# A pair's two heads in 64-row tiles of the array: scores and transposes of an attention and token-mixer kernel

## Chip, cores, metric

One Trainium2 chip, one core. The metric is the device time of one execution in microseconds (us), the median of several runs. TensorE is called PE in the profile (its weight loads PEld), VectorE DVE, ScalarE ACT, GpSimd POOL, SyncE SP.

## What is computed

q, k and v have shape (4, 8, 576, 64): four batches of eight heads, 576 positions, head size 64, fp32. The reference rotates q and k by position, takes softmax attention per head, lays the heads side by side to x of shape (4, 576, 512) and runs a token mixer and a channel mixer over it:

```python
scores = scale * np.matmul(q_rot, k_rot.transpose(0, 1, 3, 2))
scores = scores - np.max(scores, axis=-1, keepdims=True)
attn = np.exp(scores)
attn = attn / (np.sum(attn, axis=-1, keepdims=True) + 1e-09)
out = np.matmul(attn, v)
...
h = np.maximum(xt @ w_tok1, 0.0) @ w_tok2
u = x + h.transpose(0, 2, 1)
out = u + np.maximum(u @ w_ch1, 0.0) @ w_ch2
```

The mixer weights arrive as 64-bit floats and are split on the chip into rounded part and rest.

## The kernel before

The work on attention goes in 16 pairs of heads (n = 0 to 15); a pair's two heads fill the 128 partitions with 2 x 64 head columns. 576 = 512 + 64: each head has four blocks of 128 queries and a tail of 64.

`prep(n)` (from line 248) loads k, q and v of a pair (lines 258 to 265), rotates k and q (line 273; on POOL, for the first pair on DVE) and transposes them on PE: five 128x128 transposes each, lines 314 and 316. ACT writes the rounded part in fp32r from PSUM (kh, qh, line 319), DVE the rest (kl, ql, line 322). Both heads lie on top of each other then, head 0 in partitions 0 to 63, head 1 in 64 to 127. The score product wants the contraction of one head on all 128 rows: eight transfers of a pair on SP's queue (line 352) stack copies, khd = [kh; kh], kld = [kl; kl] and qs = [qh; ql] for each head. The first pair writes head 0's copies directly (lines 332 and 335).

`pair(n)` (line 385) walks nine tiles in the order of line 381: eight (head, query block) tiles and one tile (None) that holds both heads' 64 tail queries. Per tile:

- scores (line 423): four matmuls of 288 columns, (qh + ql) against kh and kl, into a score buffer of two PSUM banks; the None tile (line 414) does six against a block-diagonal bd that POOL fills (line 375);
- maximum on DVE (line 428), exponential with its sum on ACT (line 435), to p of 576 columns;
- four 128x128 transposes of p (line 445) into one PSUM bank, copied to pt by ACT or DVE (lines 453 and 455); the 64 tail columns of several tiles are transposed together later (line 465) and copied (line 485).

There are two score buffers of two banks each and four single banks for everything else, which makes up PSUM's eight banks. Twice in a pair, P times V (line 498) follows: ten fp32 products, each of which shows as two matmuls, the two heads in the lower and the upper 64 output columns of the array. The result oT is copied out (line 502), transposed back (lines 528 and 531), copied to X by ACT (line 537) and multiplied by the reciprocal sums on POOL (line 547); its 64-row tail goes through DVE (line 540).

The order of the work on each engine is fixed ahead by `Plan.run` (line 89): a list scheduler with planned durations, lags between engines and a rank from the table AT (line 144); of the tasks that can start within SLACK of the earliest one, the lowest rank goes first. A task takes its buffers when it is placed; score buffers are taken in program order. Engines then run their queues strictly in that order. The splitting of the token weights (lines 567 to 603) is spread over the first pairs on DVE, ACT and POOL. After attention come the token mixer (lines 700 and 722) and the channel mixer (lines 761, 783 and 806), which the change does not touch.

## Time and profile before

| | |
|---|---|
| median of 3 runs | 694.57 us (692.72 to 695.56) |
| the profiled execution | 693.52 us, of which the span from first to last instruction is 691.7 us |
| mean granted TensorE clock | 0.994 |
| busy share of the span | PE 95%, PEld 81%, DVE 62%, ACT 47%, POOL 42% |
| first and last P times V of attention | start at 31.6 us and 314.8 us |
| first matmul of the channel mixer's line 783 | 381.7 us |

Busy shares are unions of instruction times. Matmuls are pipelined: one that is listed with 0.3 us may be followed 0.13 us later by the next, so its cost is read from the distance of starts or from the chain of waits. The chain of waits follows the work that ended last back from the end; "issue" in it is time in which nothing recorded held the engine.

### The profile page before, as it was taken

What the parts mean: (1) busy time and instruction counts of PE and PEld (TensorE: products, weight loads), DVE (VectorE), ACT (ScalarE), POOL (GpSimd) and SP (SyncE); (2) the same over time, 40 slices, a digit from 0 to 9 for tenths busy, and PEclk for the clock granted to TensorE, in tenths of its full rate; (3) what the DMA queues carried; (4) which work ended last, traced back from release to release, by engine and by line L of the source; (5) the groups of instructions that cost most, each with busy time, mean ns of one, the idle gap of its engine ahead of it and who ended that gap; (6) DMA issues with size and microseconds to landing.
All of it is one profiled execution on the core that took longest, in us unless ns stands there. A gap on an engine that the chain in (4) does not pass through costs nothing.

```text
span 691.7 us, 11124 instructions
## 1 busy us (share of the span) xinstructions
PE 660.6 (95%) x4024; PEld 557.4 (81%) x4024; DVE 429.1 (62%) x739; ACT 324.9 (47%) x755; POOL 292.7 (42%) x314
## 2 busy tenths in 40 slices
PE   2898999999999999997999999999999999999997
PEld 1766778877777777775887989989989899899895
DVE  5789976666666666656884888727842673322322
ACT  3776777767667777764551535313411321011010
POOL 4887976666666665102832545503600340000000
PEclk9999999999999999998999999999999999999999
DMA  7665555555556654420300223202200100001212
GB/s 221 157 177 148 137 145 137 139 149 151 151 151 151 151 149 119 112 74 1 98 17 1 69 85 84 69 0 85 69 30 1 62 0 1 1 0 47 77 61 92
DMA packets 43127, 61.75 MB, mean 89 GB/s; under 512 B 11584, under 2 KB 24640, under 8 KB 43072
## 3 DMA queue, kind: packets, MB, share of 16 engines
q1 hardware_dynamic: 42528, 60.38, 32.1%
q8 instruction: 32, 0.52, 0.3%
q10 hardware_dynamic: 544, 0.66, 0.3%
q14 instruction: 23, 0.19, 0.1%
HBM read 29.88 MB, written 4.72 MB: 50 GB/s over the span
## 4 chain that ended last, share of the span: by engine, by line
PE 81%; ACT 6%; DVE 5%; issue 4%; DMA 2%; SPq 0%; POOL 0%; ACTq 0%; DVEq 0%; POOLq 0%
PE m L783 22%; PE m L806 22%; PE t L498 10%; PE s L423 7%; PE t L445 6%; PE m L700 4%; PE m L722 4%; ACT p L435 3%; DVE nm L428 2%; ACT pt L455 2%; PE s L414 2%; PE t L465 2%; PE m L761 1%; PE t L528 1%; PE t L314 1%
## 5 line engine op out<-in xcount | busy, mean ns | idle before, releaser
L428 DVE TENSOR_REDUCE nm<-s 128x1 f32<-128x576 f32 x144 | 106.6, 749 | 45.0 <-PE s L423 36.7
L785 ACT ACTIVATE gh<-m 128x384 fp32r<-128x384 f32 x72 | 35.4, 492 | 190.9 <-PE m L783 174.7
L435 ACT ACTIVATE p<-s,nm 128x576 f32<-128x576 f32 x144 | 106.9, 744 | 30.0 <-DVE nm L428 27.5
L783 PE MATMUL m<-uh,c1h 128*128 128x384 f32 x288 | 97.1, 337 | 0.0
L783 PE MATMUL m<-uh,c1l 128*128 128x384 f32 x288 | 96.7, 336 | 0.0
L783 PE MATMUL m<-ul,c1h 128*128 128x384 f32 x288 | 96.7, 336 | 0.0
L423 PE MATMUL s<-khd,qs 128*128 128x288 f32 x256 | 83.2, 341 | 5.1 <-ACT p L435 4.2
L498 PE MATMUL t<-pt,vraw 128*64 128x256 f32 (+1 forms) x640 | 85.6, 411 | 0.2 <-ACT pt L455 0.2
L806 PE MATMUL m<-c2h,gl 128*128 128x512 f32 x216 | 85.2, 394 | 0.0
L806 PE MATMUL m<-c2l,gh 128*128 128x512 f32 x216 | 85.0, 394 | 0.0
L806 PE MATMUL m<-c2h,gh 128*128 128x512 f32 x216 | 84.9, 393 | 0.0
L787 DVE SCALAR_TENSOR_TENSOR gl<-m,gh 128x384 fp32r<-128x384 f32 x72 | 39.6, 555 | 70.4 <-ACT gh L785 70.3
L808 DVE TENSOR_TENSOR X<-m,X 128x512 f32<-128x512 f32 x64 | 44.1, 690 | 58.6 <-PE m L806 58.6
L445 PE MATMUL t<-ident,p 128*128 128x128 f32 x576 | 77.5, 275 | 0.7 <-DVE XT L540 0.4
L423 PE MATMUL s<-kld,qs 128*128 128x288 f32 x256 | 72.7, 300 | 0.0
L498 PEld LDWEIGHTS t<-pt,vraw 128*64 128x64 f32 x640 | 44.0, 137 | 31.3 <-issue 5.1
L445 PEld LDWEIGHTS t<-ident,p 128*128 128x128 f32 x576 | 66.7, 141 | 2.1 <-DVE XT L540 0.9
L423 PEld LDWEIGHTS s<-khd,qs 128*128 128x128 f32 x256 | 49.3, 192 | 20.6 <-ACT p L435 12.8
L783 PEld LDWEIGHTS m<-uh,c1h 128*128 128x128 f32 x288 | 54.2, 188 | 0.9
L783 PEld LDWEIGHTS m<-ul,c1h 128*128 128x128 f32 x288 | 54.2, 188 | 0.9
L783 PEld LDWEIGHTS m<-uh,c1l 128*128 128x128 f32 x288 | 54.2, 188 | 0.0
L592 POOL TENSOR_TENSOR fa<-fc,fa 128x384 f32<-128x384 f32 (+1 forms) x23 | 27.7, 1207 | 57.7 <-DVE fa L590 57.7
(128 smaller groups left out, 1234.7 us busy)
## 6 DMA issues: line engine op xcount, KB each, us to landing
khd<-kh SPq DMA_DIRECT2D x62, 144.0 KB, 2.6
kld<-kl SPq DMA_DIRECT2D x62, 144.0 KB, 2.7
stg<-in_moe_w_ch_dram SPq DMA_DIRECT2D x16, 384.0 KB, 3.2
stg<-in_moe_w_ch_dram SPq DMA_DIRECT2D x12, 512.0 KB, 3.6
kraw<-in_k_dram SPq DMA_DIRECT2D x16, 256.0 KB, 2.9
qraw<-in_q_dram SPq DMA_DIRECT2D x16, 256.0 KB, 3.1
vraw<-in_v_dram SPq DMA_DIRECT2D x16, 256.0 KB, 3.0
out_dram<-X SPq DMA_DIRECT2D x16, 256.0 KB, 2.3
```

Source lines behind the costliest of these rows:

```text
L423: nc.tensor.matmul(sb.t[:, c, 0:W2], a, m.t[:, h, c * W2:(c + 1) * W2], start=(x == 0), stop=(x == 1))
L428: nc.vector.tensor_reduce(out=nm.t, in_=sb.t[:, :, 0:W2], axis=AX.XY, op=ALU.max, negate=True)
L435: nc.scalar.activation(out=p.t.rearrange("p (a b) -> p a b", a=2), in_=sb.t[:, :, 0:W2], func=ACTF.Exp, bias=nm.t, accum_out=l)
L445: nc.tensor.transpose(tb.t[:, j * P:(j + 1) * P], p.t[:, j * P:(j + 1) * P], ident)
L498: nc.tensor.matmul(ab.t[h * D:(h + 1) * D, 0:w], vb.t[:, h, r, :], pt[c].t[:, r, h, 0:w], start=(r == 0), stop=(r == R))
L592: mul_ = lambda e: lambda: e.tensor_tensor(out=A(), in0=C(), in1=A(), op=ALU.mult)
L700: nc.tensor.matmul(tb.t, a, m, start=(r == 0 and i == 0), stop=(r == R and i == len(lst) - 1))
L783: nc.tensor.matmul(tb.t[:, 0:N], a, m, start=(i == 0), stop=(i == len(lst) - 1))
L785: x = add("ACT", 0.49, lambda f=f, tb=tb: nc.scalar.activation(out=gb.t[0][:, f], in_=tb.t[:, 0:N], func=ACTF.Relu), [x], [tb, gb], pr + f)
L787: y = add("DVE", 0.56, lambda f=f, tb=tb: nc.vector.scalar_tensor_tensor(out=gb.t[1][:, f], in0=tb.t[:, 0:N], scalar=0.0, in1=gb.t[0][:, f ...
L806: nc.tensor.matmul(tb.t, a, m, start=(i == 0), stop=(i == len(lst) - 1))
L808: y = add("DVE", 0.69, lambda u=u, tb=tb: nc.vector.tensor_tensor(out=u, in0=tb.t, in1=u, op=ALU.add), [z] + sums.get((ci, x), []), [tb], ...
```

## The change

Head 0 lies in the upper 64 rows and head 1 in the lower 64 rows of kh, kl, qh and ql, and the scores are now computed from there, each head in its own 64-row tile of the array, with three products (qh kh, qh kl, ql kh) in place of the stacked two matmuls. One task (0.8 us in the plan) computes the block of 128 queries for both heads: 12 matmuls of 288 columns, head 0 and head 1 alternating, into both score buffers. khd, kld, qs and their transfers are gone; kh, kl, qh and ql have two buffers each.

All transposes of attention (k and q, p, oT) are done as two half transposes, rows 0 to 63 and rows 64 to 127, each of 128 stationary columns against a 64x64 identity, into two PSUM banks; what was one bank and one copy becomes two banks and two copies of 64-column blocks. The key blocks are laid out so that head 0's tail keys and head 1's tail keys are neighbours: p of both heads is one tile of 1152 columns, and the block of both tails is transposed with head 1's. k's and q's 64 tail rows are loaded into both partition halves, v's into one half per head with zeros in the other. The final multiplication by the reciprocal sums is done by DVE out of PSUM; ACT's copy and POOL's multiplication go.

The plan gets a mode per PE task (full, row or col) and 0.15 us where the mode changes. The None tile's scores stay in full mode.

```diff
+        want = {}
...
-                if not sl.free or (sl.fifo and b.order != sl.taken):
+                k = want[sl] = want.get(sl, -1) + 1
+                if len(sl.free) <= k or (sl.fifo and b.order != sl.taken + k):
                     return None
-                s = max(s, min(sl.free)[0])
+                s = max(s, sorted(sl.free)[k][0])
+        if eng == "PE" and t.mode != self.mode:
+            s = max(s, self.clock["PE"] + SWITCH)
         return s
...
+            if eng == "PE":
+                self.mode = t.mode
...
+SWITCH = 0.15
...
-        hls = {x: slots(x, 1, [P, S], F32R) for x in ("kh", "kl", "qh", "ql")}
-        khds = slots("khd", 2, [P, 2, S], F32R)
-        klds = slots("kld", 2, [P, 2, S], F32R)
-        qss = slots("qs", 2, [P, 2, M], F32R)
+        hls = {x: slots(x, 2, [P, 2 * R + 2, TL], F32R) for x in ("kh", "kl", "qh", "ql")}
         bds = slots("bd", 2, [P, 2, P], F32R)
-        ps = slots("p", 4, [P, S])
-        pts = slots("pt", 3, [P, R + 1, 2, 2 * P + TL])
-        oTs = slots("oT", 2, [P, S])
+        ps = slots("p", 3, [P, 2 * S])
+        pqs = slots("pq", 1, [P, S + TL])
+        pts = slots("pt", 3, [P, 2 * R + 1, 2 * P + TL])
+        oTs = slots("oT", 2, [P, M + P])
...
+        for j in range(4):
+            nc.scalar.dma_start(out=tabs[TL:P, j, R], in_=tab[j, 0:TL, R])
...
-                def dup(dst, o, h, src, w):
-                    def go():
-                        nc.sync.dma_start(out=dst.t[o * D:(o + 1) * D, h, 0:w].bitcast(F32),
-                                          in_=src.t[h * D:(h + 1) * D, 0:w].bitcast(F32))
...
+                    xy = [Buf(t_ps), Buf(t_ps)]
+
+                    split = r0 > 0
+                    first = int(n > 0)
+
+                    def tr(r0=r0, r1=r1, xy=xy, ub=ub, first=first):
+                        for i in range(r1 - r0):
+                            for z in range(2):
+                                r = (i - 1) % (R + 1) if z and first else r0 + i
+                                nc.tensor.transpose(xy[z].t[:, i * TL:(i + 1) * TL],
+                                                    ub.t[halves[z], r].rearrange("p h d -> p (h d)"), ident[halves[z], halves[z]])
+
+                    pp = pos + AT["pt"] + pr if n else FIRST + r0
+                    t = add("PE", 0.11 * (r1 - r0), tr, x, [*xy, ub, hi, lo], pp, mode="row")
+                    for z in range(2):
+                        m = r1 - r0 - (z and split)
+                        i0 = 0 if z and first else 2 * r0 + z + 1
+                        parts = [(0, m, i0)] + ([(m, 1, 0)] if z and split else [])
+                        for o, m, i0 in parts:
+                            src = lambda z=z, xy=xy, m=m, o=o: xy[z].t[:, o * TL:(o + m) * TL].rearrange("p (r s) -> p r s", s=TL)
+                            at = lambda d, i0=i0, m=m: d.t[:, i0:i0 + 2 * m - 1:2]
+
+                            def fh(hi=hi, src=src, at=at):
+                                nc.scalar.copy(out=at(hi), in_=src())
+
+                            def fl(hi=hi, lo=lo, src=src, at=at):
+                                nc.vector.tensor_tensor(out=at(lo), in0=src(), in1=at(hi), op=ALU.subtract)
+
+                            y = add("ACT", act(m * TL), fh, [t], [xy[z], hi], pp)
+                            eh.append(y)
+                            el.append(add("DVE", dve(m * TL), fl, [y], [xy[z], hi, lo], pp))
+                ready[n, nm] = (eh + el, hi, lo)
...
+                                nc.gpsimd.tensor_copy(out=bb.t[halves[h], o, halves[h]], in_=src.t[halves[h], 2 * R + 1])
+                            bdone.append(add("POOL", 0.3, cp, eh + el, [bb, src], pp))
...
-        ORDER = [(0, 0), (1, 0), (0, 1), (1, 1), None, (0, 2), (1, 2), (0, 3), (1, 3)]
-        ORDER0 = [(0, 0), (0, 1), (0, 2), (0, 3), (1, 0), (1, 1), None, (1, 2), (1, 3)]
+        ORDER = [0, 1, None, 2, 3]
...
+            for i, j in enumerate(ORDER):
+                g = 9 * n + 2 * i
+                c = 0 if j in (0, 1) else 1
+                if j is None:
...
+                                nc.tensor.matmul(sb.t[:, c, 0:W2], a, flat(m.t)[:, TL + c * W2:TL + (c + 1) * W2], start=(x == 0), stop=(x == 2))
+                    x = add("PE", 0.81, qk, bdone + kd, [sb, bb, kh, kl], g + AT["qkt"])
...
+                    def tr(pb=pb, xy=xy):
+                        for r in range(R + 1):
+                            for z in range(2):
+                                c0 = r * P - (TL if z and r == R else 0)
+                                nc.tensor.transpose(xy[z].t[:, r * TL:(r + 1) * TL], pb.t[halves[z], c0:c0 + P], ident[halves[z], halves[z]])
+
+                    x = order_tr[0] = add("PE", 0.55, tr, [*x, order_tr[0]], [*xy, pb, pt[c]], g + AT["tr"], mode="row")
+                    y = None
+                    for z in range(2):
+                        def cp(e, z=z, xy=xy, c=c, m=R + 1 - z):
+                            return lambda: e(out=pt[c].t[:, (R + 1) * z:(R + 1) * z + m, 2 * P:2 * P + TL],
+                                             in_=xy[z].t[:, 0:m * TL].rearrange("p (r s) -> p r s", r=m))
+
+                        y0, y = y, both(cp, (R + 1 - z) * TL, [x], [xy[z], pt[c]], g + AT["cp"])
+                        ev[c].append(y)
+
+                    def cpt(e, xy=xy, c=c):
+                        return lambda: e(out=pt[c].t[halves[1], R, 2 * P:2 * P + TL], in_=xy[1].t[halves[1], R * TL:(R + 1) * TL])
+                    ev[c].append(both(cpt, TL, [x, y0], [xy[1], pt[c]], g + AT["cp"]))
...
+                sbs, nmb, pb = [Buf(s_ps), Buf(s_ps)], [Buf(nms), Buf(nms)], Buf(ps)
+
+                def qk(sbs=sbs, j=j):
+                    for c in range(2):
+                        for x, (a, m) in enumerate(((qh, kh), (qh, kl), (ql, kh))):
+                            for h in range(2):
+                                nc.tensor.matmul(sbs[h].t[:, c, 0:W2], flat(a.t)[halves[h], TL + j * P:TL + (j + 1) * P],
+                                                 flat(m.t)[halves[h], TL * (1 - h) + c * W2:TL * (1 - h) + (c + 1) * W2], start=(x == 0), stop=(x == 2))
+                t = add("PE", 0.8, qk, qd + kd, [*sbs, qh, ql, kh, kl], g + AT["qk"], mode="row")
+                xs = []
+                for h in range(2):
+                    x = add("DVE", 0.67, mx(sbs[h], nmb[h]), [t], [sbs[h], nmb[h]], g + h + AT["mx"])
+                    x = add("ACT", 0.65, ex(sbs[h], nmb[h], lambda h=h, pb=pb: pb.t[:, h * S:(h + 1) * S], lambda h=h, j=j: lb.t[:, j, h:h + 1]), [x],
+                            [sbs[h], nmb[h], pb, lb], g + h + AT["ex"])
+                    xs.append(x)
+                exps += xs
+                o = j % 2 * P
+
+                for h in range(2):
+                    xy = [Buf(t_ps), Buf(t_ps)]
+                    m = R + h
+
+                    def tr(pb=pb, xy=xy, h=h, m=m):
+                        for i in range(m):
+                            for z in range(2):
+                                c0 = h * M + i * P
+                                nc.tensor.transpose(xy[z].t[:, i * TL:(i + 1) * TL], pb.t[halves[z], c0:c0 + P], ident[halves[z], halves[z]])
+
+                    x = order_tr[0] = add("PE", 0.11 * m, tr, [*xs[0:h + 1], order_tr[0]], [*xy, pb, pt[c]], g + h + AT["tr"], mode="row")
+                    for z in range(2):
+                        def cp(e, z=z, xy=xy, c=c, o=o, h=h, m=m):
+                            return lambda: e(out=pt[c].t[:, R * h:R * h + m, o + z * TL:o + (z + 1) * TL],
+                                             in_=xy[z].t[:, 0:m * TL].rearrange("p (r s) -> p r s", r=m))
+                        ev[c].append(both(cp, m * TL, [x], [xy[z], pt[c]], g + h + AT["cp"]))
+                if j not in (1, 3):
...
-                            nc.tensor.matmul(ab.t[h * D:(h + 1) * D, 0:w], vb.t[:, h, r, :], pt[c].t[:, r, h, 0:w],
-                                             start=(r == 0), stop=(r == R))
+                            m = pt[c].t[:, R if r == R else r + h * (R + 1), 0:w]
+                            nc.tensor.matmul(ab.t[halves[h], 0:w], vb.t[:, h, r, :], m, start=(r == 0), stop=(r == R))
...
+                x = add("PE", 10 * (w / 1200 + 0.0025), pv, ev[c] + vdone, [ab, vb, pt[c]], g + AT["pv"], mode="col")
...
+            xy = [Buf(t_ps), Buf(t_ps)]
...
-                for j in range(R):
-                    nc.tensor.transpose(tb.t[:, j * P:(j + 1) * P], oT.t[:, j * P:(j + 1) * P], ident)
...
-            def f6():
-                nc.scalar.copy(out=xm, in_=tb.t.rearrange("p (r c) -> p r c", r=R))
...
-            def f8():
-                x4 = xm.rearrange("p r (h d) -> p r h d", h=2)
-                nc.gpsimd.tensor_tensor(out=x4, in0=x4, in1=rb.t[:, 0:R, :].unsqueeze(3).to_broadcast([P, R, 2, D]), op=ALU.mult)
...
+                for j in range(R + 1):
+                    for z in range(2):
+                        nc.tensor.transpose(xy[z].t[:, j * D:(j + 1) * D], oT.t[halves[z], j * P:(j + 1) * P], ident[halves[z], halves[z]])
+
+            x = add("PE", 0.55, f4, pv_done, [*xy, oT], pp, mode="row")
+            for z in range(2):
+                def f5(z=z):
+                    nc.vector.tensor_tensor(out=X[b][:, :, cs + z * D:cs + (z + 1) * D], in0=xy[z].t[:, 0:R * D].rearrange("p (r d) -> p r d", r=R),
+                                            in1=rb.t[:, 0:R, z].unsqueeze(2).to_broadcast([P, R, D]), op=ALU.mult)
+
+                def f6(z=z):
+                    nc.vector.tensor_tensor(out=tail_of(b)[:, cs + z * D:cs + (z + 1) * D], in0=xy[z].t[0:TL, R * D:(R + 1) * D],
+                                            in1=rb.t[0:TL, R, z:z + 1].to_broadcast([TL, D]), op=ALU.mult)
+                x_done.setdefault(b, []).append(add("DVE", dve(R * D), f5, [x, inv], [xy[z], rb], pp + AT["f6"]))
+                x_done[b].append(add("DVE", dve(D), f6, [x, inv], [xy[z], rb], pp + AT["f6"] + 0.1))
```

## Rows read from the trace of the kernel before

**Rows 1.** The page: busy time of the engines over the span.

```profile
PE 660.6 (95%) x4024; PEld 557.4 (81%) x4024; DVE 429.1 (62%) x739; ACT 324.9 (47%) x755; POOL 292.7 (42%) x314
```

**Rows 2.** Windows: length, then busy us and instructions of PE, PEld, DVE, ACT, POOL.

```profile
119.05:283.17 164.12, 162.44 (x1243) 129.16 (x1242) 107.67 (x199) 117.10 (x289) 101.86 (x124) 1.00 0.55 140
35.68:82.86 47.18, 41.94 (x305) 32.47 (x304) 43.47 (x63) 35.17 (x89) 40.02 (x40) 1.00 0.59 151
```

**Rows 3.** Chain of waits over one pair: start, us, engine, tile, line, instructions.

```profile
200.86 2.31 PE t L498 x20
203.16 1.25 PE s L423 x8
...
204.53 1.31 PE t L445 x12
...
210.47 2.84 PE t L498 x20
...
214.64 0.53 PE s L423 x4
...
219.14 0.36 PE t L498
```

**Rows 4.** Timeline of PE, first 0.34 us of one P times V.

```profile
200.78 0.44 PE L498 MATMUL t<-pt,vraw 128*64 128x256 f32 x2
```

**Rows 5.** Timeline of weight loads, the first two after P times V.

```profile
203.09 0.19 PEld L423 LDWEIGHTS s<-khd,qs 128*128 128x128 f32 x1 [0.39 <-issue]
...
203.20 0.19 PEld L423 LDWEIGHTS s<-kld,qs 128*128 128x128 f32 x1
```

**Rows 6.** Timelines: the hand-offs from scores to maximum, exponential and next scores.

```profile
297.89 0.40 PE L423 MATMUL s<-khd,qs 128*128 128x288 f32 x1 [0.19 <-ACT p L435]
...
298.40 0.29 PE L423 MATMUL s<-kld,qs 128*128 128x288 f32 x1
...
298.80 0.76 DVE L428 TENSOR_REDUCE nm<-s 128x1 f32<-128x576 f32 x1 [0.23 <-ACT pt L455]
...
299.59 0.74 ACT L435 ACTIVATE p<-s,nm 128x576 f32<-128x576 f32 x1
...
215.85 1.43 DVE L428 TENSOR_REDUCE nm<-s 128x1 f32<-128x576 f32 x2
...
289.46 0.74 ACT L435 ACTIVATE p<-s,nm 128x576 f32<-128x576 f32 x1 [0.46 <-DVE nm L428]
...
290.34 0.19 PEld L423 LDWEIGHTS s<-khd,qs 128*128 128x128 f32 x1
```

**Rows 7.** Groups by form, ACT and DVE: count, busy us, mean ns, idle before.

```profile
L455 ACT COPY pt<-t 128x512 f32<-128x512 f32 x63 | 35.2, 588 | 4.0 <-PE t L445 3.0
...
L319 ACT CAST kh<-t 128x320 fp32r<-128x320 f32 x16 | 6.9, 432 | 0.3
...
L322 DVE TENSOR_TENSOR ql<-t,qh 128x320 fp32r<-128x320 f32 x16 | 7.8, 490 | 30.2 <-ACT qh L319 30.1
...
L322 DVE TENSOR_TENSOR ql<-t,qh 128x256 fp32r<-128x256 f32 x16 | 6.7, 421 | 2.5 <-ACT qh L319 2.4
...
L485 ACT COPY pt<-t 64x256 f32<-64x256 f32 x18 | 6.7, 370 | 1.0 <-PE t L465 0.2 <-DVE pt L485 0.2
```

**Rows 8.** Chain of waits in the first pairs.

```profile
31.17 0.59 SPq L352
...
33.47 2.55 DMA kld<-kl
```

**Rows 9.** Chain and timeline: second P times V of three pairs, then the last multiplication.

```profile
82.93 2.87 PE t L498 x20
...
283.24 2.84 PE t L498 x20
...
314.78 3.10 PE L498 MATMUL t<-pt,vraw 128*64 128x320 f32 x20
...
319.54 1.04 POOL L547 TENSOR_TENSOR X<-X,ri 128x512 f32<-128x512 f32 x1 [3.00 <-ACT X L537]
```

More of the change, by code (lines that the diff above doesn't have):

```diff
@@ L49 @@
 class Task:
-    __slots__ = ("alts", "deps", "bufs", "prio", "end", "eng", "waits", "heirs")
+    __slots__ = ("alts", "deps", "bufs", "prio", "end", "eng", "waits", "heirs", "mode")
 LAG = {"PE": 0.2, "ACT": 0.14, "DVE": 0.12, "POOL": 0.12, "SP": 1.8}
@@ L62, in __init__, with add @@
         self.slack = SLACK
-    def add(self, eng, dur, fn, deps=(), bufs=(), prio=0.0, alts=()):
+        self.mode = None
+    def add(self, eng, dur, fn, deps=(), bufs=(), prio=0.0, alts=(), mode="full"):
         t = Task()
+        t.mode = mode
         t.alts = [(eng, dur, fn)] + list(alts)
@@ L241, in attention, with both @@
             nc.gpsimd.memset(t[TL:P, R, 1:2], 1.0)
-        for _, _, t in pts.free:
-            nc.gpsimd.memset(t[TL:P, R], 0.0)
-        make_identity(nc, ident)
-        ready_q, ready_k, ready_v, kpair, bd_of = {}, {}, {}, {}, {}
+        for _, _, t in raw["v"].free:
+            nc.gpsimd.memset(t[TL:P, 0, R, :], 0.0)
+            nc.gpsimd.memset(t[0:TL, 1, R, :], 0.0)
+        for _, _, t in oTs.free:
+            nc.gpsimd.memset(t[:, S:M + P], 0.0)
+        for _, _, t in pqs.free:
+            nc.gpsimd.memset(t[:, S:S + TL], 0.0)
+        make_identity(nc, ident)
+        ready, ready_v, bd_of = {}, {}, {}
+        order_tr = [None]
+        halves = (slice(0, TL), slice(TL, P))
+        def both(fn, n, deps, bufs, prio):
+            return add("ACT", act(n), fn(nc.scalar.copy), deps, bufs, prio, alts=[("DVE", dve(n), fn(nc.vector.tensor_copy))])
         def prep(n):
@@ L250, in prep @@
             pos = 9 * n
-            hb = {}
-            last = []
             for nm, src, pr in (("k", k, 0.0), ("q", q, 0.5), ("v", v, 1.0)):
@@ L388, in pair @@
             pt = [Buf(pts) for _ in range(2)]
[L389 to L392 removed]
+            kd, kh, kl = ready[n, "k"]
+            qd, qh, ql = ready[n, "q"]
             bdone, bb = bd_of[n]
             vdone, vb = ready_v[n]
[L395 to L397 removed]
@@ L398, in pair @@
-            place = lambda t: (1, 2 * P) if tiles[t] is None else (tiles[t][1] // 2, tiles[t][1] % 2 * P)
-            ends = {max(t for t in range(9) if place(t)[0] == c): c for c in range(2)}
-            def both(fn, n, *args, prio):
-                return add("ACT", act(n), fn(nc.scalar.copy), *args, prio, alts=[("DVE", dve(n), fn(nc.vector.tensor_copy))])
+            flat = lambda t: t.rearrange("p r s -> p (r s)")
+            ev = {0: [], 1: []}
+            exps = []
             oT = Buf(oTs)
@@ L405, in pair, with mx, ex @@
             pv_done = []
-            for t in range(9):
-                g = 9 * n + t
-                sb = Buf(s_ps)
-                if tiles[t] is None:
+            def mx(sb, nm):
+                return lambda: nc.vector.tensor_reduce(out=nm.t, in_=sb.t[:, :, 0:W2], axis=AX.XY, op=ALU.max, negate=True)
+            def ex(sb, nm, p, l):
+                return lambda: nc.scalar.activation(out=p().rearrange("p (a b) -> p a b", a=2), in_=sb.t[:, :, 0:W2], func=ACTF.Exp,
+                                                    bias=nm.t, accum_out=l())
@@ L413, in qk @@
                             for x, (a, m) in enumerate(passes):
-                                nc.tensor.matmul(sb.t[:, c, 0:W2], a, m[:, c * W2:(c + 1) * W2], start=(x == 0), stop=(x == 2))
-                    x = add("PE", 0.81, qk, bdone + keh + kel, [sb, bb, khi, klo], g + AT["qk"])
-                else:
-                    h, j = tiles[t]
-                    def qk(sb=sb, h=h, j=j):
-                        a = qb.t[:, h, j * P:(j + 1) * P]
-                        for c in range(2):
-                            for x, m in enumerate((khd, kld)):
-                                nc.tensor.matmul(sb.t[:, c, 0:W2], a, m.t[:, h, c * W2:(c + 1) * W2], start=(x == 0), stop=(x == 1))
-                    x = add("PE", 0.55, qk, qdone[h] + kdone[h], [sb, qb, khd, kld], g + AT["qk"])
```

172 lines of the change are left out of this document (22 added, 150 removed).

## The prediction

> **What bounds the kernel now.** I read the page first: PE is busy for 95% of the span, no other engine for more than 62% [rows 1]. A busy PE is no proof of a bound, since matmuls overlap in the records, so the second view is the chain of waits over one pair in the even middle of attention [rows 3]. It goes from one P times V to the next in 219.14 - 200.86 = 18.28 us and consists almost wholly of PE's own work. The pitches in it are: 12 transposes in 1.31, so 0.109 each; 4 score matmuls in 0.53, so 0.133 each; P times V 2.31 and 2.84. These two differ by 0.53 for 10 x 64 columns, so 10 steps of 256 columns need 2.12, and entering this mode costs about 0.19. The eight score matmuls behind it take 1.25 where 8 x 0.133 = 1.06, so leaving it costs another 0.19.
>
> PE's work in a pair is then 32 score matmuls x 0.133 = 4.26, six of the None tile 0.80, 60 transposes (45 of p, 10 of k and q, 5 of oT) x 0.109 = 6.54, and P times V 2.31 + 2.84 + 2 x 0.19 = 5.53: together 17.13 of 18.28. PE binds, with 1.15 us of standing still in a pair. In the windows view DVE works 107.67 / 9 = 12.0 and ACT 117.10 / 9 = 13.0 us of nine such pairs [rows 2]: loaded, not full. Eleven steps of this pace lie between the second P times V of pair 3 at 82.93 and that of pair 14 at 283.24 [rows 9], 18.21 each. Before them, DVE is busy 43.47 of 47.18 us with the token weights beside attention [rows 2], and the pace is slower. The mixers behind attention are not changed.
>
> **The change part by part.**
>
> *Scores.* Four blocks of six steps replace 32 matmuls, a step being one matmul for each head. Whether the two heads run side by side in row tiles no row shows. The nearest row is P times V, whose two heads lie in column tiles: two matmuls start inside the first 0.34 us as one record of 0.44 [rows 4], and ten steps of two products take 2.31. The best case for a score step is 0.133, the streaming of 288 columns; the worst is 0.22, if two loads of 128 columns follow each other: behind P times V the second load starts 203.20 - 203.09 = 0.11 after the first [rows 5]. I take 0.133, by the column tiles: 24 x 0.133 = 3.19, a gain of 1.07.
>
> The full-size scores also show that a load and the matmul ahead of it overlap: 0.133 is less than a load of 0.11 plus 288 columns of streaming. The Trainium skill, TensorE: Matmul & The Clock Gate, section Part 3 (The mechanism), says that weight loads overlap running matmuls only when their row groups differ. The trace's full-array scores do not agree with it; by that rule alone a step would be a load and a stream in turn, an estimated 0.23, PE's work would come above 21 us a pair, and the change would lose.
>
> *Transposes.* 36 + 5 half pairs of p, 10 of k and q and 5 of oT make 56 steps for 60. A step streams half the columns (0.055 at best) but loads 128 stationary columns, 0.11 [rows 5]; the worst is 0.22. I take 0.109, the load's: 56 x 0.109 = 6.10, a gain of 0.44.
>
> *Modes.* The None tile's full-array scores now sit between row tiles. The row for a change of mode is P times V's entry and exit, 0.38 together; bounds 0 to 0.38; I take 0.38. P times V and the None scores stay.
>
> PE's work: 3.19 + 0.80 + 6.10 + 5.53 + 0.38 = 16.0, or 1.13 less than today.
>
> *The score buffers* are the new chain. A block now takes both buffers at once, so the next block waits for both exponentials. With the hand-offs of today [rows 6]: six steps until the last starts take 0.10 + 0.66 (the first pitch is longer), the maximum starts 298.80 - 298.40 = 0.40 behind the last start, two maxima take 1.43, the exponential follows a maximum at 0.03 and takes 0.74, and PE restarts 290.34 - 290.20 = 0.14 behind it. The first exponential ends at 2.69, the second at 3.43, the next block starts at 3.57. The None tile takes the first buffer that comes free, at 2.83, and needs 1.16 + 0.76 + 0.03 + 0.74 + 0.14 of its own and some 0.19 for the mode, so that the next block starts 5.85 behind the last one. A pair is 3 x 3.57 + 5.85 = 16.6 us at least. That is above PE's 16.0: score buffers, DVE and ACT become the bound.
>
> *Lateness.* Each of the five starts can be late when DVE or ACT is in a copy. Such copies take 0.43 to 0.49 [rows 7], on average half of one, 0.2, is left. 16.6 + 5 x 0.2 = 17.6; bounds 0 and a whole copy, 0.49.
>
> *Copies on ACT and DVE.* For p, nine of 512 columns (0.588) and tails of about 1.6 become 16 of 256 or 320 (0.37 and 0.43) and three for the None tile: 6.9 to 7.45. The rounded part and rest go to 320 columns throughout, +0.27. ACT's copy to X goes, -0.59; DVE takes two multiplications of 256 (0.42 each) and two of 64 (0.2, an estimate from these) for one of 128 (0.28), +0.96. Together +1.2 on 25.0 us of two engines; they have 35 in a pair, so it costs only through lateness.
>
> *Queues.* SP issues eight transfers less and three tail loads more per pair; the copies' landing matters once, in the first pair, where the chain stands from 31.17 to 36.02 on four issues and a landing [rows 8]. That is 4.8 us; DVE, full there, gets the work of the wait back and has 1 us more a pair. I take half, -2.5; bounds -4.8 and +3. Four small loads on ACT's queue at the start hide behind the first rotation. POOL's multiplication goes from the end of attention, 1.04 [rows 9] for 0.84 on DVE and no copy of 0.59: -0.8. POOL's bd copies now wait for all eight splits of q; ranks well ahead of the None tile cover it, and without that cover it is one 0.5 us start a pair, inside the lateness.
>
> *The end.* The last two steps take 314.78 - 283.24 = 31.5 us today, since there is no preparation left beside them [rows 9]. The score chain does not shrink with it: 17.6 + 16.6 = 34.2, +2.7.
>
> **The sum**: 11 x (17.6 - 18.21) = -6.7, -2.5, -0.8, +2.7: -7.3 us. Against the profiled execution's 693.52 (span 691.7) this gives 686.2; the median of the runs stands 1.05 higher, so 687.
>
> **The rivals.** *The buffer chain holds without lateness* (16.6): 11 x -1.6 = -17.7, -4.8, -0.8, +1.7: 673. For it: DVE and ACT have a quarter of their time free; the scheduler ranks scores and exponentials first. Against: PE's 16.0 must fit between the blocks without delaying one, and P times V is 3 us in one piece where a block leaves 2.7.
>
> *It is lost again in the buffers.* With a lateness of 0.33 per start (half a copy on DVE and a little on ACT) a pair is at 18.2 and only start and end differ: about 695.
>
> *Slower by the same chain.* One whole copy, 0.49, ahead of each start: 16.6 + 2.45 = 19.05, 11 x 0.84 = +9.2, end +6.5 - 0.8, first steps -2.5: 707. It decides from 0.33 on. For it: both engines run strictly in the planned order, the block's maxima and exponentials stand in it among some 27 other instructions of a pair, and the plan counts 0.67 and 0.65 for what takes 0.76 and 0.74. The Trainium skill, TensorEngine Tiling (Array Packing), section PSUM Bottleneck, says the same in general: tiling speeds up TensorE, not the emptying of PSUM, which may become the bottleneck.
>
> *The tiles do not run side by side.* 24 and 56 steps at 0.22: PE's work is 5.3 + 12.3 + 0.80 + 5.53 + 0.38 = 24.3 a pair: 11 x 6.1 = +67, +8 in the first three steps, +15 in the last two: about 784. Loads that wait for their own tile's stream end near there too (21 us a pair, some 740). Against both: the column tiles [rows 4] and the pitch of the full array [rows 3].
>
> **How the numbers follow.** Half a percent, 3.5 us, is about what a measurement of this kernel can tell from no change. Forecast and its near side (678 to 691) 0.36; the chain without lateness (under 678) 0.20; nothing to be seen (691 to 698) 0.18; slower by the chain 0.20; tiles one after the other 0.06. That gives faster 0.56, same 0.18, slower 0.26. The range goes from 668, five below the best case, since its hand-offs are single rows, to 708, the slower chain: some 0.15 is left out, most of it above. The likeliest cases' own range is 673 to 691.
>
> **What would show it.** Right: pairs of score matmuls of the two heads that start within 0.01 us, a step of 0.13, transposes at 0.11 per two; PE's gaps ahead of scores ended by ACT's exponential, some 3.6 to 4 us apart; a pair at 17 to 18 us; no transfers of khd, kld and qs. Wrong: a score step of 0.22 or more; a pair under 16.6, which would mean that scores started without waiting for both buffers; PE still without gaps.

## The result, and the profile after

The change makes the kernel **slower by 0.9%**: 699.51 us median (696.52 to 701.61, 13 runs) against 693.07 (691.86 to 695.56, 13 runs) of the kernel before in the same comparison, ratio 1.0086, 95% interval 1.0071 to 1.0101. The forecast was 687. The profiled execution after took 696.52 us, span 694.7, where that of before took 693.52 and 691.7: the traces differ by 3.0 of the 6.4 us.

The edit also gives the new kernel another rank table AT and other values of SLACK ("qk" goes from -1.07 to -239.14, for example), which the section on the change does not say. So the 0.9% belongs to row tiles and another order together, and only the runs below that choose the order anew on both sides take the two apart.

The page first, the line that answers to [rows 1]:

```profile
PE 630.0 (91%) x5112; PEld 529.2 (76%) x5112; DVE 432.4 (62%) x807; ACT 319.8 (46%) x808; POOL 282.1 (41%) x304
```

PE's busy time went down by 30 us and no other engine's went up by more than 3.3. The windows view over nine even pairs, and over the two steps from the second P times V of pair 1 to that of pair 3, for [rows 2]:

```profile
119.87:285.55 165.68, 145.07 (x1854) 112.67 (x1855) 109.43 (x235) 116.05 (x325) 92.75 (x115) 1.00 0.18 49
39.09:80.80 41.71, 34.80 (x424) 27.67 (x423) 38.19 (x68) 31.04 (x85) 36.50 (x39) 0.94 0.26 73
```

The two early steps take 41.71 us for 47.18, but they begin 3.4 us later (39.09 for 35.68). Nine even pairs take 1.56 us longer, and PE is busy for 17 us less of them: it waits, and neither DVE nor ACT is full. DMA's share fell from 0.55 to 0.18 and bought nothing. The timeline of the second P times V, for [rows 9], at pairs 3, 4, 14 and 16:

```profile
80.80 3.38 PE L467 MATMUL t<-pt,vraw 128*64 128x320 f32 x20
...
101.48 0.89 PE L467 MATMUL t<-pt,vraw 128*64 128x320 f32 x3
...
285.55 3.23 PE L467 MATMUL t<-pt,vraw 128*64 128x320 f32 x20
...
320.76 3.63 PE L467 MATMUL t<-pt,vraw 128*64 128x320 f32 x20
```

Pair 3 comes 2.1 us earlier than before (82.93), pair 14 comes 2.3 later (283.24), pair 16 comes 6.0 later (314.78). So attention loses 4.4 us in the eleven steps, (285.55 - 80.80) / 11 = 18.61 instead of 18.21, of which ten are even at 18.41 and the first takes 20.68, and 3.7 in the last two. That makes 6 us at the last P times V, of which what follows gives 3 back.

Where an even pair loses it is seen in the chain of waits (start, us, engine, tile, line), for [rows 3]:

```profile
199.60 1.07 PE s L396 x6
...
200.76 0.77 DVE nm L379
...
201.56 0.84 ACT pq L382 x2
...
202.44 0.95 PE s L429 x10
...
203.41 0.76 DVE nm L379
204.17 0.33 DVE pt L413
...
204.53 0.24 DVE pt L420
...
204.79 0.77 DVE nm L379
...
205.65 0.84 ACT p L382 x2
...
206.53 0.99 PE s L429 x11
```

In [rows 3] the chain was all PE. Now it goes from scores to a maximum on DVE, an exponential on ACT and back to scores: the two score buffers set the pace. Between the two maxima of the block at 202.44 stand two copies, L413 and L420. The next part of the pair, the timelines of PE and then of ACT and DVE (start, us, engine, line):

```profile
210.12 0.38 PE L429 MATMUL s<-kh,qh 64*128 64x288 f32 x1
...
211.92 3.33 PE L467 MATMUL t<-pt,vraw 128*64 128x320 f32 x20
215.18 0.40 PE L429 MATMUL s<-kh,qh 64*128 64x288 f32 x2
```
```profile
211.81 0.48 DVE L454 COPY pt<-t 128x320 f32<-128x320 f32 x1
...
212.72 0.74 ACT L341 CAST qh<-t 128x320 fp32r<-128x320 f32 x2
...
213.98 0.22 ACT L382 ACTIVATION_READ_ACCUMULATOR p<-s,nm 128x1 f32 x1
```

The last exponential of the block at 210.1 has read its buffer at 214.2, yet the next scores start at 215.18: P times V stands ahead of them in PE's queue. The exponential is itself some 0.7 later than the prediction's hand-offs give, since a copy (L454) stands between the block's two maxima on DVE and two roundings of q (L341) between its exponentials on ACT. The five starts of a pair are 2.84 (to None), 2.84, 4.09, 3.57 and 5.08 apart, 18.42 in all (the start of a block is taken where both heads' products run). Against the prediction's floor, 3 x 3.57 + 5.85 = 16.56, None and its successor lie 0.17 below, the start behind L413 and L420 is 0.52 late, and the one behind P times V 1.51.

### The profile page after: what moved, and what is told of

Its sections match the earlier page's. It is cut to its first block, busy times and chain, and to the rows that moved or that the text cites. A ratio compares the mean times of both kernels' runs of the same rounds, so it can differ in the third digit from the quotient of the medians.

```text
span 694.7 us, 13160 instructions
## 1 busy us (share of the span) xinstructions
PE 630.0 (91%) x5112; PEld 529.2 (76%) x5112; DVE 432.4 (62%) x807; ACT 319.8 (46%) x808; POOL 282.1 (41%) x304
## 4 chain that ended last, share of the span: by engine, by line
PE 74%; DVE 12%; ACT 9%; issue 2%; DMA 2%; SPq 0%; DVEq 0%; ACTq 0%
PE m L738 22%; PE m L761 22%; PE s L429 8%; PE t L467 8%; DVE nm L379 6%; ACT p L382 4%; PE m L677 4%; PE m L655 4%; PE t L449 4%; ACT pt L454 2%; DVE pt L454 2%; ACT pq L382 2%; PE s L396 1%; PE m L716 1%; DVE X L501 1%
## 5 line engine op out<-in xcount | busy, mean ns | idle before, releaser
L379 DVE TENSOR_REDUCE nm<-s 128x1 f32<-128x576 f32 x144 | 105.0, 749 | 71.2 <-PE s L429 68.3
L382 ACT ACTIVATE p<-s,nm 128x576 f32<-128x576 f32 x128 | 94.5, 741 | 14.4 <-DVE nm L379 12.3
L467 PE MATMUL t<-pt,vraw 128*64 128x256 f32 (+1 forms) x640 | 92.6, 413 | 2.0 <-DVE pt L454 0.2
L429 PE MATMUL s<-kh,qh 64*128 64x288 f32 x256 | 64.0, 352 | 17.9 <-ACT pq L382 14.1
L454 ACT COPY pt<-t 128x256 f32<-128x256 f32 (+1 forms) x160 | 57.9, 396 | 39.6 <-PE t L449 38.1
L467 PEld LDWEIGHTS t<-pt,vraw 128*64 128x64 f32 x640 | 57.0, 138 | 24.7 <-ACT pt L454 5.0
L449 PE MATMUL t<-ident,p 64*128 64x64 f32 x1152 | 60.0, 230 | 13.7 <-ACT p L382 6.4
L449 PEld LDWEIGHTS t<-ident,p 64*128 64x128 f32 x1152 | 52.9, 143 | 20.7 <-ACT p L382 14.7
L429 PEld LDWEIGHTS s<-kh,qh 64*128 64x128 f32 x256 | 37.8, 194 | 38.7 <-ACT pq L382 17.6
L429 PE MATMUL s<-kl,qh 64*128 64x288 f32 x256 | 52.4, 316 | 0.0
```

The source lines that it names most:

```text
L379: return lambda: nc.vector.tensor_reduce(out=nm.t, in_=sb.t[:, :, 0:W2], axis=AX.XY, op=ALU.max, negate=True)
L382: return lambda: nc.scalar.activation(out=p().rearrange("p (a b) -> p a b", a=2), in_=sb.t[:, :, 0:W2], func=ACTF.Exp, bias=nm.t, accum_ou ...
L429: nc.tensor.matmul(sbs[h].t[:, c, 0:W2], flat(a.t)[halves[h], TL + j * P:TL + (j + 1) * P], flat(m.t)[halves[h], TL * (1 - h) + c * W2:TL ...
L449: nc.tensor.transpose(xy[z].t[:, i * TL:(i + 1) * TL], pb.t[halves[z], c0:c0 + P], ident[halves[z], halves[z]])
L454: return lambda: e(out=pt[c].t[:, R * h:R * h + m, o + z * TL:o + (z + 1) * TL], in_=xy[z].t[:, 0:m * TL].rearrange("p (r s) -> p r s", r=m))
L467: nc.tensor.matmul(ab.t[halves[h], 0:w], vb.t[:, h, r, :], m, start=(r == 0), stop=(r == R))
```

## The experiments

Theory A: the chain of the two score buffers sets the pace, lengthened by what the order of the queues puts between its links. B: the more numerous copies on ACT and DVE limit. C: PE's own work still does. The first four are the changed kernel with one edit each; the first three of them ran once.

**scores_twice**: each block of scores is computed two times.

```diff
-                    for c in range(2):
+                    for c in (0, 0, 1, 1):
```

> Each block of scores is computed twice over (24 more steps of a pair, 0.131 each, same results, same order of tasks). Theory A, the chain of the two score buffers sets the pace (scores, two maxima, second exponential, next scores): each of the four blocks is 0.79 us later, a pair takes 18.4 + 3.1 = 21.5 us, the run about 699 + 16 x 3.1 = 749 us. Rival B, DVE and ACT with the more numerous copies set the pace: PE has about 5 us idle in a pair, so next to nothing, 699 to 705 us. Rival C, PE's own work sets the pace: +3.1 a pair as in A; the next run tells A from C.

742.62 us, span 740.7. The even step goes from 18.41 to 21.58, by 3.17; the added 24 steps at 0.131 are 3.14. All of it shows, so scores lie on the path: A or C, not B.

**trans_twice**: each half transposition of p is done two times.

```diff
-                        for i in range(m):
+                        for i in [i for i in range(m) for _ in range(2)]:
...
-                        for r in range(R + 1):
+                        for r in [r for r in range(R + 1) for _ in range(2)]:
```

> Each half transpose of p is done twice over (41 more steps of a pair, 0.061 each = 2.5 us of PE work, same results, same order). Theory A: the transposes lie beside the maxima and exponentials; only those that stand in PE's queue ahead of P times V and of the next scores count, so 0 to 1 us a pair, 699 to 715 us. Rival C, PE's work sets the pace: +2.5 a pair, about 739 us. Rival B, copies set the pace: copies start later by up to 0.3 in places, 699 to 705 us.

710.27 us, span 708.5; step 19.07, by 0.66 more, for 41 added steps of two half transposes, which are about 2.5 us of PE's work. Three quarters of it lay in PE's waits. That speaks against C.

**pv_short**: the second P times V of a pair sums two blocks instead of five.

```diff
-                    for r in range(R + 1):
+                    for r in range(R + 1) if c == 0 else (0, R):
```

> The second P times V of each pair keeps only its first and last of five blocks of keys (12 of 20 matmuls left out, so that part of the sum over keys is missing for half of the queries); the order of tasks stays. Theory A: the scores behind it wait for it 0.96 us longer than for the exponentials (215.18 against 214.08 + 0.14), so a pair takes 17.4 to 17.5 and the run is 13 to 16 us shorter, 684 to 687 us. Rival C, PE's work sets the pace: 1.6 us a pair, 674 us. Rival B: no change, 699 us.

684.1 us, span 682.1, step 17.36. Its P times V of 320 columns takes 1.72 us for 3.33, and 1.05 of this comes off the step: about what stands between the end of the exponential (214.2) and the next scores (215.18). B has no place for that, and C would have taken off all 1.6.

**max_together**: the second maximum of a block is issued right behind the first, ahead of the copies that the order had put between them (the instructions are issued from a list once all are planned, and the list is changed first).

```diff
...
+            if tag[0] == "mx1" and i > at[("mx0",) + tag[1:]]:
+                after[at[("mx0",) + tag[1:]]] = i
+                gone.add(i)
...
```

> In DVE's queue each second maximum of a block is moved up to directly behind the first one; everything else keeps its order. Theory A in its simple form (what stands between the two maxima is what the pair loses): the two copies of 0.57 us between the maxima of block 2 go behind, block 2 becomes 3.57 instead of 4.09, a pair 17.9, the run 691 to 693 us. Rival B: the same copies are late at their next user instead (P times V of the pair or the transposes' banks), a pair stays at 18.3 to 18.6, the run at 697 to 703 us.

701.76 us (700.48 to 702.03), ratio 1.0124 (1.0104 to 1.0143): no gain. The timeline shows why, at the same place of a pair:

```profile
206.81 0.40 PE L450 MATMUL s<-kh,qh 64*128 64x288 f32 x1 [0.89 <-ACT pq L403]
...
210.42 0.40 PE L450 MATMUL s<-kh,qh 64*128 64x288 f32 x2
...
214.12 0.37 PE L450 MATMUL s<-kh,qh 64*128 64x288 f32 x1
...
217.02 2.90 PE L489 MATMUL t<-pt,vraw 128*64 128x320 f32 x18 [0.34 <-DVE pt L476]
219.85 0.40 PE L450 MATMUL s<-kh,qh 64*128 64x288 f32 x2
```

The start that was 4.09 behind is now 3.61 behind, as A wanted. But in the next block the copy that was moved behind the second maximum (L476 here, L454 above) feeds P times V: 18 of its 20 matmuls wait for it until 217.02, and the scores behind it come 5.73 after their block instead of 5.08. The gain of 0.48 goes into a loss of 0.65, and a pair takes 18.71. So moving the copies alone gains nothing while the long P times V stands ahead of the scores.

The order of all queues comes from the numbers in AT and SLACK. The next four kernels have these chosen anew, each kernel for itself, by a count of the planned order with the durations and hand-offs that the traces show.

**after_ranks**: the changed kernel, only these numbers differ. They also decide which of ACT and DVE makes a copy, where either may.

```diff
-AT = {"qk": -239.14, "mx": 17.16, "ex": -436.59, "tr": -5.68, ...
+AT = {"qk": -13.3267, "mx": 13.59742, "ex": 6.16432, "tr": 10.47856, ...
...
-SLACK = {"PE": 0.08, "ACT": 0.06, "DVE": 0.32, "POOL": 0.17, "SP": 0.05}
+SLACK = {"PE": 0.48578, "ACT": 0.04086, "DVE": 3.16736, "POOL": 0.04556, "SP": 0.05}
```

> The changed kernel with other numbers in AT and SLACK, so that only the order of the instructions differs. They were chosen with the durations and hand-off times that the trace of after shows in the place of the listed costs. Theory A (the pace is the chain of the two score buffers, and what the old ranks put in its way: the P*V of 320 columns ahead of the next scores, copies between the two maxima, 1.85 us per pair over the floor of 16.6): a count of the new order gives a step of 17.2 to 17.4 us per pair instead of 18.41, 14 steps of about 1.1 us, 684 (679 to 690) instead of 699.5. Theory B (VectorE and ScalarE with their more numerous copies limit): the same copies in another order, 697 to 703. Theory C (PE's own work): the same work, 697 to 703.

686.53 us (685.1 to 686.92), ratio to before 0.9897 (0.9873 to 0.9922): 13 us under after with the same work (DVE has 821 instructions for 807, ACT 789 for 808). B and C fall. But a pair takes 17.70 at best, 0.3 over A's count, and 18.2 on average, and the windows view shows a new loss (us, PE, PEld, DVE, ACT and POOL busy, granted clock, DMA share, GB/s):

```profile
221.80:224.70 2.90, 2.29 (x43) 2.00 (x41) 2.41 (x6) 1.96 (x6) 2.75 (x4) 1.00 0.40 113
224.70:227.50 2.80, 2.21 (x25) 1.68 (x26) 2.06 (x5) 2.46 (x8) 2.72 (x3) 1.00 0.13 25
227.50:229.70 2.20, 2.20 (x23) 2.08 (x22) 1.27 (x3) 0.39 (x1) 2.14 (x4) 0.53 0.45 129
229.70:233.20 3.50, 3.50 (x23) 1.63 (x22) 1.50 (x4) 1.99 (x5) 0.48 (x3) 0.81 0.00 0
```

Behind two stretches in which PE was busy for 2.29 of 2.90 and 2.21 of 2.80 us, the granted clock fell to half, 1.2 GHz. A score step took 0.24 instead of 0.13. There are six such falls in this attention. That suggests a theory D: a PE that is left waiting loses its clock. Waiting alone does not decide it: from 100 to 280 us PE is busy for 159.11 us here and for 157.98 in after, where the clock stays whole.

**before_ranks**: the kernel before, with AT and SLACK chosen in the same way.

> The control for after_ranks: the kernel before with AT and SLACK chosen in the same way. Theory A says that before was held by PE's own work (178.2 us busy of 180), so that another order gives little in the middle: the count gives a step of 17.3 us where the same count gives 17.95 for the old order and the trace shows 18.21; 686 (681 to 692). If PE's work in before is as dense as its busy share says, no gain: 691 to 695. If it gains as much as after_ranks (15 us or more, 678 or less), the order and not the change sets the time in both.

685.3 us (684.82 to 685.81), ratio 0.9884 (0.9861 to 0.9906), an even step of 17.31:

```profile
100.00:280.00 180.00, 179.97 (x1434) 148.33 (x1435) 123.21 (x220) 134.06 (x346) 117.61 (x144) 1.00 0.55 143
```

PE is now busy without a gap, and 17.31 is close to the 17.13 that the prediction counted as its work. The kernel before had 0.9 us of waits per pair to lose as well. With the order chosen anew on both sides, the change is worth nothing as it stands (686.5 against 685.3); in after_ranks the falls of the clock are in that sum.

**after_split_ranks**: the scores of a block become two tasks, one for each head with one score buffer.

```diff
...
-                t = add("PE", 0.8, qk, qd + kd, [*sbs, qh, ql, kh, kl], g + AT["qk"], mode="row")
...
+                    t = add("PE", 0.8, lambda h=h, qk=qk: qk(h), qd + kd, [sbs[h], qh, ql, kh, kl], g + h + AT["qk"], mode="row")
...
```

> After, with the scores of a block as two tasks, one for each head, each with one score buffer (the two heads' matmuls no longer alternate), and ranks chosen as in after_ranks. It undoes the one part that asks for both buffers at once and keeps the rest. PE's own work rises by 24 steps of 0.131 = 3.1 us per pair, from about 13.5 to 16.6. Theory A: each buffer is refilled as soon as its own exponential has read it, the step is PE's 16.9 by the count, 682 (677 to 690): no slower than after_ranks although PE works 3.1 us more. Theory C (PE's own work sets the pace, at 18.41 already): 18.41 + 3.1, 735 to 745. A third outcome: 64-row matmuls that alternate no longer do not hide their weight loads (0.131 becomes about 0.19 each): step about 19.5, 710 to 720.

692.29 us (688.65 to 698.53, 10 runs), ratio 0.9997 (0.9961 to 1.0034). There are 3.1 us more of PE's work per pair, and yet an even step takes 17.5 to 17.7, under after's 18.41: C falls for good. The third outcome did not come either: score matmuls that no longer alternate keep their pitch of 0.13 (last section). The median is 10 us over A's number all the same: the even steps are 0.6 to 0.8 over the counted 16.9, and the first pairs are slow, with the clock at half from 50 to 60 and from 88 to 101 us.

**before_half_ranks**: one part alone on the kernel before, p transposed in halves. It has its own AT and SLACK, and the transposes of k and q now take the buffers of their results (hi, lo) in advance, as in the changed kernel.

```diff
...
-                    for j in range(R):
-                        nc.tensor.transpose(tb.t[:, j * P:(j + 1) * P], p.t[:, j * P:(j + 1) * P], ident)
+                    for j in range(R):
+                        for z in range(2):
+                            hz = slice(z * TL, (z + 1) * TL)
+                            nc.tensor.transpose(xy[z].t[:, j * TL:(j + 1) * TL], p.t[hz, j * P:(j + 1) * P], ident[hz, hz])
...
```

> The kernel before with one part of the change alone: p is transposed in halves, two 64-row tiles into two banks (0.061 us for two instead of 0.109 for a whole one), and copied out as twice as many copies of half the columns; scores, stacked copies and tail stay as before. Ranks chosen in the same way. Theory A: before was held by PE, 36 steps of 0.048 = 1.7 us per pair come off it, scores still take one buffer at a time: step 16.7 by the count, 681 (676 to 688), under both kernels and under before_ranks by about 5. Theory B (more numerous copies cost what PE gains): no better than before_ranks, 686 or more.

698.2 us (697.65 to 700.66), ratio 1.0076 (1.0048 to 1.0105), even step 18.31: A's number is missed by 17 us. PE's timeline, one visit to the half transposes between full-array scores:

```profile
208.92 0.29 PE L425 MATMUL s<-kld,qs 128*128 128x288 f32 x1
209.14 0.47 PE L449 MATMUL t<-ident,p 64*128 64x64 f32 x8
209.54 0.40 PE L425 MATMUL s<-khd,qs 128*128 128x288 f32 x1
209.77 0.29 PE L425 MATMUL s<-kld,qs 128*128 128x288 f32 x1
```

The first transposes start 0.22 behind the last score instead of 0.13, and the scores behind them have a first pitch of 0.23 instead of 0.13. From 208.92 to 209.77 it is 0.85; whole transposes would take 0.133 + 4 x 0.109 + 0.133 = 0.70. Eight such visits in a pair are 1.2 us, and 18.31 is 1.0 over before_ranks. PE is busy for 177.78 of 180 us, so B's copies do not explain it: here, changing between full array and row tiles costs more than four half transposes save. In the changed kernel, where the scores around them are row tiles too, half transposes start 0.13 behind the last score (216.08 behind 215.95).

**after_ranks_fill**: after_ranks, with the transposes of q's rotation and of oT done two times (the cut shows oT's).

```diff
...
-                for j in range(R + 1):
+                for j in [j for j in range(R + 1) for _ in range(2)]:
```

> after_ranks with two groups of transposes done twice (those of q's rotation and those of oT; the second pass writes the same values to the same place): 0.6 us more of PE's work per pair, put where PE waits in any case (0.36 before the scores of j = None, 0.57 after the transposes of oT in the trace of after_ranks). Theory D, new: in after_ranks the granted clock falls to half six times for some 3.3 us (at 40, 98, 135, 173, 227 and 309 us), each time beside PE's longest waits, and the pairs with a fall take 18.6 to 19.5 us instead of 17.70; with the waits filled the falls go, all pairs take 17.7, about 6 times 1.3 us, 679 (677 to 683). Rival: the falls are not due to those waits, they stay, and the extra work costs what it displaces, 686 to 692.

681.64 us (680.06 to 682.14), ratio 0.9837 (0.9818 to 0.9856): 4.9 us under after_ranks by doing more. The clock is whole from 46 us on and the late pairs take 17.69 each; two falls stay in the first pairs, and two pairs between 110 and 148 us still take 17.9 to 18.5 with the clock whole, which D does not explain. D is borne out in the main: the other falls went when the waits were filled, and the time came down inside its bounds. That another shift of PE's work would have done the same was not tried.

**after_pv_ranks**: each P times V becomes two tasks, r = 0 and 1, then r = 2 to 4, so that scores can go between them; own AT and SLACK.

```diff
...
-                x = add("PE", 10 * (w / 1200 + 0.0025), pv, ev[c] + vdone, [ab, vb, pt[c]], g + AT["pv"], mode="col")
+                x = None
+                for rs in ((0, 1), (2, 3, 4)):
+                    x = add("PE", 2 * len(rs) * (w / 1200 + 0.0025), lambda pv=pv, rs=rs: pv(rs), ev[c] + vdone + [x], [ab, vb, pt[c]], g + AT["pv"], mode="col")
```

> After, with each P*V as two tasks (blocks r = 0, 1 and r = 2 to 4, in the same bank), so that the scores of a block can go between them, and with ranks of its own chosen as in after_ranks. Theory A: the P*V of 320 columns stood ahead of the scores of the next block (5.08 us from block to block where the chain needs 3.57); with that gone the count gives a step of 16.6 us per pair, the floor of the chain of score buffers; with the lateness that after_ranks showed over its count (0.3) 16.9, 9 us under after_ranks: 677 (674 to 681) if the clock holds. Theory D: PE waits more in every pair, the clock falls as often as in after_ranks or more, and takes back 6 to 10 us: 683 to 690. Theory B: 697 or more.

**674.29 us** (673.68 to 675.21), ratio 0.9736 (0.9719 to 0.9754), as A had it. PE's timeline:

```profile
205.54 1.30 PE L467 MATMUL t<-pt,vraw 128*64 128x320 f32 x8
...
207.21 0.85 PE L429 MATMUL s<-kh,qh 64*128 64x288 f32 x2
...
208.96 1.83 PE L467 MATMUL t<-pt,vraw 128*64 128x320 f32 x12
...
212.93 2.38 PE L467 MATMUL t<-pt,vraw 128*64 128x256 f32 x20
```

A block of scores goes out between the two pieces of the 320 columns. From one P times V of 256 columns to the next, 196.06 to 212.93, a pair takes 16.87, against the floor of 16.56. This beats before and after, and before_ranks by 11 us. What of the 12 us under after_ranks is the split's is not taken apart: after_pv_ranks has an order of its own (DVE has 765 instructions for 821, ACT 848 for 789) and one fall of the clock before 297 us where after_ranks has five, and after_ranks with these numbers but without the split was not run. The even pairs, 16.87 for 17.70, make up most of it. A split P times V in the kernel before was not tried either; there PE has no gap left in the even pairs.

**after_pv_fill**: the same filling on after_pv_ranks.

> after_pv_ranks with the transposes of q's rotation and of oT done twice as in after_ranks_fill. Theories A and D together: 676 (672 to 680), under after_pv_ranks wherever that one shows falls of the clock. If the clock has no part: equal to after_pv_ranks or up to 5 us over it.

674.15 us (673.52 to 675.88), ratio 0.9738 (0.9715 to 0.9762): no difference. The clock of after_pv_ranks stays whole between 60 and 296 us already, so the theories say the same here and the run does not tell them apart.

## Why the prediction was wrong

*What bounds before*: PE, but with more waits around it than the 1.15 us looked like costing: the order alone gave 0.9 of them back (before_ranks, 17.31 for 18.21).

*Scores*: right. In PE's timeline of after, each row holds the matmuls of both heads:

```profile
202.68 0.42 PE L429 MATMUL s<-kh,ql 64*128 64x288 f32 x2
202.82 0.41 PE L429 MATMUL s<-kh,qh 64*128 64x288 f32 x2
202.95 0.41 PE L429 MATMUL s<-kl,qh 64*128 64x288 f32 x2
```

The two heads start at most 0.014 apart (0.06 in the block at 210.1), and behind a first pitch of 0.24 steps follow at 0.13. The Trainium skill, TensorE: Matmul & The Clock Gate, section Part 3, says that weight loads overlap matmuls only of other row groups. By that a step would have been an estimated 0.23; these rows do not agree with it.

*Transposes*: mis-sized. Two half transposes take 0.06, not 0.109: in after, from 216.08 on, nine steps of two follow each other at 0.062, near the 0.055 that the prediction gave as the best case. Its load of 0.11 did not set the pace: the loads of the two row tiles start within 0.005 of each other, and the pairs of loads follow at 0.06 too. PE's work is therefore about 13 us a pair (3.14 + 0.80 + 56 x 0.06 + 5.53), not 16.0, and nothing came of it, since the buffers bind.

*Modes*: 0.38 was taken for None's full-array scores. In the even pairs it is hidden, as PE waits there for an exponential (the None start is not late). The cost itself is real, as before_half_ranks shows.

*The score buffers*: right, and the core of the matter. Of the five starts of a pair two come at the forecast distance, the one behind None 0.18 before it, and after_pv_ranks runs at 16.87 for the floor of 16.6.

***Lateness* is the step that failed.** "Each of the five starts can be late when DVE or ACT is in a copy", 0.2 each, 1.0 in all. It was 1.86, in two starts only: 0.52 behind copies and 1.51 at the start behind P times V, less the 0.17 at None. Of the 1.51, 0.8 to 1.0 is PE's own queue, where the prediction had no lateness (pv_short took 1.05 off the step), and the rest is copies on DVE and ACT. The text named P times V as "3 us in one piece where a block leaves 2.7" and put it only into a rival. In the changed kernel P times V starts 1.8 us behind the block's first score and the next scores start 3.26 behind it, 5.08 together where the chain needs 3.57. That makes the step 18.41 instead of 17.6, and so longer than the 18.21 of before, not shorter. It lies between the rivals "lost again in the buffers" (18.2) and "slower by the same chain" (19.05), for another reason than the one that they give.

*Copies*: +1.2 us a pair was counted on DVE and ACT together; nine pairs show 225.5 us for 224.8, 0.1 a pair.

*The first pairs*: -2.1 at pair 3 for -2.5, but not in the way that was forecast, so the closeness is luck. The gain was to come in the first pair, where the copies' landing is gone; the second P times V of pair 1 starts 3.4 later than before (39.09 for 35.68) and that of pair 2 only 0.2 earlier (61.31 for 61.52). These pairs also lost clock, as the last section shows. Behind pair 3 one step took 20.68, 2.3 more than the even ones. The trace of after shows most of it on DVE, where three pieces of the token weights' splitting stand ahead of the maximum of the block that starts at 90.03:

```profile
89.53 1.14 DVE L541 TENSOR_SCALAR fa<-fa 128x128 uint32<-128x128 uint32 x1
90.70 0.86 DVE L543 SCALAR_TENSOR_TENSOR fh<-stg,fa 128x128 uint32<-128x128 uint32 x1
91.59 1.52 DVE L545 TENSOR_SCALAR fa<-fh 128x128 uint32<-128x128 uint32 x1
93.03 0.74 DVE L379 TENSOR_REDUCE nm<-s 128x1 f32<-128x576 f32 x1
```

The maximum starts 3.00 behind its block's start, where it is 0.97 in an even pair (203.41 behind 202.44).

*The end*: +3.7 up to the last P times V, for +2.7. Behind it, up to the channel mixer's first matmul, 64.0 us follow instead of 66.9, where the prediction had -0.8 for POOL's multiplication. Two things differ there. The matmul from which the token mixer runs on starts 5.8 us behind the last P times V (326.60) for 7.9 (322.70), without POOL in the chain. And TensorE's granted clock stands at half for 3.4 us instead of 6.8, by the windows of before and after:

```profile
321.51:328.34 6.83, 5.80 (x14) 4.51 (x14) 6.33 (x13) 1.16 (x2) 1.85 (x1) 0.50 0.01 2
...
327.14:330.55 3.41, 3.41 (x9) 2.63 (x9) 3.38 (x6) 1.72 (x4) 3.41 (x2) 0.50 0.00 0
```

No run varied either.

The sum by the same terms: 11 x 0.40 = +4.4 instead of -6.7, -2.1 for -2.5, -3.0 for -0.8 and +3.7 for +2.7. That is +3.0, the difference of the two profiled executions, where -7.3 was forecast.

The Trainium skill, TensorEngine Tiling (Array Packing), section PSUM Bottleneck, says that tiling speeds up TensorE but not the emptying of PSUM, which may become the bottleneck. The trace agrees in so far as the score buffers set the pace: DVE waits for scores, PE for exponentials, and neither DVE nor ACT is full. How much it costs was a matter of the order and of P times V's length in one piece, 699.5 or 674.3 us.

## What to carry to other kernels

When a change moves the bound from an engine to a chain of hand-offs, look at what stands in each queue ahead of the chain's links: a long task just ahead of a link holds the link up until it ends, and cutting it in two, with an order to fit, gave more here than the change itself. Compare two versions each with an order fitted to it; a list of ranks that suits one program says little about another. Work taken off an engine that does not bind buys nothing, and the waits that it leaves may cost clock.

## What the chip showed that was not expected

PE's clock can fall when PE is left waiting. These are the windows of after that hold PE's waits of 1.70 and 1.81 us in the first pairs, each with the one behind it, where the clock falls to half:

```profile
33.15:35.88 2.73, 0.99 (x22) 0.71 (x18) 2.73 (x5) 2.45 (x8) 2.50 (x3) 1.00 0.19 50
35.88:39.09 3.21, 3.14 (x41) 2.81 (x41) 2.49 (x6) 1.65 (x6) 1.90 (x2) 0.68 0.23 45
...
54.24:56.89 2.65, 0.84 (x23) 0.73 (x20) 2.58 (x5) 1.37 (x4) 0.96 (x2) 1.00 0.28 73
56.89:60.06 3.17, 2.94 (x31) 2.61 (x32) 2.41 (x6) 3.12 (x11) 2.94 (x4) 0.59 0.28 84
```

Before had no such fall between 25 us, when its score steps go from 0.24 to 0.13, and 321 us. In after_ranks much shorter waits went with a fall in some pairs and not in others of the same order, and in after two waits of about 1 us between 93 and 97 us lost no clock; what decides is not shown here.

A row tile left free is used by whatever comes next in the queue. In after_split_ranks the matmuls of one head run beside half transposes:

```profile
212.71 0.29 PE L429 MATMUL s<-kh,ql 64*128 64x288 f32 x1
212.72 0.27 PE L449 MATMUL t<-ident,p 64*128 64x64 f32 x1
212.84 0.29 PE L429 MATMUL s<-kh,qh 64*128 64x288 f32 x1
212.85 0.27 PE L449 MATMUL t<-ident,p 64*128 64x64 f32 x1
```

The scores keep their pitch of 0.13, so the transposes beside them cost them nothing.
